# A decode layer on one core: another form for the load of x, and another pad ahead of the buffers

## The chip, the cores and the metric

The kernel runs on one core of one Trainium2 chip. The metric is the time of one execution on the device in microseconds. Before the change the median of three runs is 193.54 us (193.43 to 193.62).

## What is computed

One token (x is 1 x 1 x 512, bf16) goes through a layer norm. From the normed x come an attention over the last 4096 positions of a cache with 32 heads of 128, and a small MLP with two inner products whose result gates the attention's output. All inputs are bf16.

```python
def _A_ref(x, k_cache, v_cache, wq, wo):
    W = min(4096, max(256, Sk // 4))            # 4096
    q = (x @ wq).reshape(B, Sq, Hq, Dh).transpose(0, 2, 1, 3)
    k = k_cache[:, :, Sk - W:, :]
    v = v_cache[:, :, Sk - W:, :]
    scores = jnp.einsum("bhqd,bhkd->bhqk", q, k) * (Dh ** -0.5)
    o = jnp.einsum("bhqk,bhkd->bhqd", _softmax(scores), v)
    return o.transpose(0, 2, 1, 3).reshape(B, Sq, Hq * Dh) @ wo

def _B_ref(x, w1, w2, w3, w4):
    ...
    x1 = x + hs                                  # hs: shifted h @ w2; with one token the shift leaves zeros
    h2 = _gelu(_layernorm(x1) @ w3) @ w4
    return x1 + h2

xn = _layernorm(x)
s = _A_ref(xn, A_k_cache, A_v_cache, A_wq, A_wo)
g = _silu(_B_ref(xn, B_w1, B_w2, B_w3, B_w4))
return x + s * g
```

K and V of the window are 33.6 MB each, the weights that are read some 12 MB more.

## The kernel before

**Tiling.** The 32 heads are worked in 8 groups of `G = 4`. A group's K, and likewise its V, is one tile of 128 partitions x 128 positions x 128 numbers, 32 KB in each partition, 4.19 MB in all. K has three buffers in `k_pool`, V two in `v_pool`. The pool `v_pool` is opened only when the second K group is through, in the place of the pool `wts`, which holds the weights of q and of the MLP and the tiles that are used at the start alone.

**x.** It is loaded twice: `x_bf` (L78, L79), spread as columns over 128 partitions with four numbers in each, and `x_row` (L80 to L82), as four rows of 128 in partitions 0, 32, 64 and 96 of a tile that GpSimd has cleared. `x_bf` is cast to `x_f` (L183) and goes into the layer norm (`ln_stats`, L158 to L179: two products with a matrix of ones on PE, the rest on DVE, one power on GpSimd). Out come `xn_f` and `xn_bf`. `x_row` is used by `xn_row` (L242) and for the output at the very end (L656).

**From x to q.** `xn_bf` is permuted by a product (`xq_ps`, L194, `xq_bf`, L196) and multiplied with `wq_sb` into two PSUM tiles `qr_ps` (L208), which are copied to `q_row` (L210 on ACT, L211 on DVE), spread to all partitions by a product with `sel` (L214) into `q_bc` (L216), and turned into `q_pair` (L218 to L226).

**The MLP** runs beside it: 16 small products with `w2_sb` (L233), a second layer norm, products with `w3_sb` (L252), Gelu on ACT (L255), products with `w4_sb` (L270), and the gate `g_row` (L280).

**The groups.** For 64 or 80 of a group's 128 columns DVE multiplies K with q (`prod`, L321) and sums (`S`, L323) in four parts; the others are transposed on PE (`pt`, L339), copied by ACT (`kt`, L342) and multiplied on PE (`sT`, L350). Softmax and the products with V (`ov`, L427) follow two groups behind. Of the last group V comes in three pieces, and the last piece is multiplied one position column at a time (`oT`, L461); then come the output rows with wo (`y_ps`, L155), the gate (L654), x (L656) and the store.

**Queues and order.** SP issues all loads of the caches and of most weights, in program order (`load`, L75, L76): `w2_sb`, `w3_sb`, `w4_sb` in two parts, K of group 0 in two halves, then K and V in turn. ACT's queue issues `x_bf`, `x_row` and `wq_sb`, in this order. Engines work in order, each on its own list. The setup up to the loop over the groups is put in order by a scheduler; from L529 on the order of PE, DVE and ACT is the one written out by hand. Each transfer counts up one of eight completion semaphores, which are given out in turn; a transfer that takes one over waits until the earlier transfer that had it has landed. In the kernel before, SP's second K half takes over that of `x_bf`, the second K group that of `w2_sb`, the third that of `x_row`. The constants of the setup (`ident_bf`, `sel`, `perm`, and the masks of `make_masks`, L128 to L141) are made by GpSimd and DVE.

**Places in memory.** Pools lie behind one another. The pool `small` begins with a tile `pad` of 192 bytes (L71), then `x_bf` (8 bytes, which take 32), then `x_row` and the rest; behind `small` lie the pool `sm` and then `wts` or `v_pool`. `k_pool` lies ahead of them all.

Of the kernel before, what the change touches and what calls it, by code (L numbers as in the profile page):

```python
# [8 lines left out]
P = 128  # L9
BF16 = mybir.dt.bfloat16  # L10
FP32 = mybir.dt.float32
ACT = mybir.ActivationFunctionType
ALU = mybir.AluOpType
AX = mybir.AxisListType
# [12 lines left out]
def kernel(  # L27
# [14 lines left out]
    nc = tc.nc  # L42

    Bb, Sq, D = A_x.shape
    assert Bb == 1 and Sq == 1, "decode kernel: B == Sq == 1"
    _, H, Sk, Dh = A_k_cache.shape
    HD = A_wq.shape[1]
# [6 lines left out]
    KC = D // P  # L54
# [9 lines left out]
    small = ctx.enter_context(tc.tile_pool(name="small", bufs=1))  # L64
    ps_misc = ctx.enter_context(tc.tile_pool(name="ps_misc", bufs=1, space=PSUM))
# [2 lines left out]
    ps_o = ctx.enter_context(tc.tile_pool(name="ps_o", bufs=1, space=PSUM))  # L68
    ps_y = ctx.enter_context(tc.tile_pool(name="ps_y", bufs=1, space=PSUM))
    sm_pool = ctx.enter_context(tc.tile_pool(name="sm", bufs=3))  # L70
    small.tile([P, 96], BF16, name="pad")  # L71
    wts_guard = tc.tile_pool(name="wts", bufs=1)
    wts = wts_guard.__enter__()

    def load(dst, src):  # L75
        return tc.keep_in_program_order(nc.sync.dma_start(out=dst, in_=src))  # L76

    x_bf = small.tile([P, KC], BF16, name="x_bf")  # L78
    nc.scalar.dma_start(out=x_bf[:], in_=A_x.rearrange("a b (p c) -> p (a b c)", p=P))  # L79
    x_row = small.tile([P, P], BF16, name="x_row")  # L80
    nc.gpsimd.memset(x_row[:], 0.0)
    nc.scalar.dma_start(out=x_row[0:P:32, :], in_=A_x.rearrange("a b (j n) -> (a b j) n", j=KC))  # L82
    wq_sb = wts.tile([P, KC, HD], BF16, name="wq_sb")
    nc.scalar.dma_start(out=wq_sb[:].rearrange("p c n -> p (c n)"),
                        in_=A_wq.rearrange("(a b c) n -> b a (c n)", a=4, c=KC))
    w2_sb = wts.tile([P, KC, D], BF16, name="w2_sb")
    load(w2_sb[:], B_w2.rearrange("(p c) n -> p c n", p=P))
    w3_sb = wts.tile([P, KC, F], BF16, name="w3_sb")
# [14 lines left out]
    ident_bf = const.tile([P, P], BF16, name="ident_bf")  # L103
# [54 lines left out]
    def ln_stats(src_f, tag):  # L158
        ps = ps_misc.tile([P, KC], FP32, tag="misc", name="ln_ps")
        nc.tensor.matmul(ps[:], lhsT=ones_f[:], rhs=src_f, start=True, stop=True)  # L160
        tot = small.tile([P, 1], FP32, name=f"ln_tot_{tag}")
        nc.vector.reduce_sum(out=tot[:], in_=ps[:], axis=AX.X)
        negmean = small.tile([P, 1], FP32, name=f"ln_negmean_{tag}")
        nc.vector.tensor_scalar(out=negmean[:], in0=tot[:], scalar1=-1.0 / D,
                                scalar2=None, op0=ALU.mult)
        xc = small.tile([P, KC], FP32, name=f"ln_xc_{tag}")
        nc.vector.tensor_scalar(out=xc[:], in0=src_f, scalar1=negmean[:], scalar2=None,
                                op0=ALU.add)
        sq = small.tile([P, KC], FP32, name=f"ln_sq_{tag}")
        nc.vector.tensor_tensor(out=sq[:], in0=xc[:], in1=xc[:], op=ALU.mult)  # L170
        ps2 = ps_misc.tile([P, KC], FP32, tag="misc", name="ln_ps2")
        nc.tensor.matmul(ps2[:], lhsT=ones_f[:], rhs=sq[:], start=True, stop=True)
        vtot = small.tile([P, 1], FP32, name=f"ln_vtot_{tag}")
        nc.vector.reduce_sum(out=vtot[:], in_=ps2[:], axis=AX.X)
        rstd = small.tile([P, 1], FP32, name=f"ln_rstd_{tag}")
        nc.vector.tensor_scalar(out=rstd[:], in0=vtot[:], scalar1=1.0 / D,
                                scalar2=LN_EPS, op0=ALU.mult, op1=ALU.add)
        nc.gpsimd.tensor_tensor(out=rstd[:], in0=rstd[:], in1=neg_half[:, 0:1], op=ALU.pow)
        return xc, negmean, rstd  # L179


    x_f = small.tile([P, KC], FP32, name="x_f")
    nc.vector.tensor_copy(out=x_f[:], in_=x_bf[:])  # L183
    xc, negmean, rstd = ln_stats(x_f[:], "x")
    xn_f = small.tile([P, KC], FP32, name="xn_f")
    nc.vector.tensor_scalar(out=xn_f[:], in0=xc[:], scalar1=rstd[:], scalar2=None, op0=ALU.mult)
# [16 lines left out]
    for b in range(2):  # L203
        zeros(qr[b][:])
        for c in range(KC):
            wc = wq_sb[:, c, :].rearrange("p (g a d) -> p g a d", a=G, d=Dh)
            for a in range(G):
                nc.tensor.matmul(qr[b][32 * a:32 * a + 1], lhsT=xq_bf[:, c:c + 1], rhs=wc[:, 4 * b:4 * b + 4, a, :],  # L208
                                 start=False, stop=(c == KC - 1), skip_group_check=True)
    nc.scalar.copy(out=q_row[:, 0:4, 0, :], in_=qr[0][:])  # L210
    nc.vector.tensor_copy(out=q_row[:, 4:8, 0, :], in_=qr[1][:])  # L211
    for b in range(2):
        qb_ps = ps_tr.tile([P, 4, Dh], FP32, tag="pt", name="qb_ps")
        nc.tensor.matmul(qb_ps[:], lhsT=sel[:].rearrange("k b a -> k (b a)"), rhs=q_row[:, 4 * b:4 * b + 4, 0, :],  # L214
                         start=True, stop=True)
        nc.scalar.copy(out=q_bc[:, 4 * b:4 * b + 4, :], in_=qb_ps[:])  # L216
    for b in range(2):
# [5 lines left out]
        for t in range(2):  # L223
            rows = slice(64 * t, 64 * t + 64)
            nc.scalar.copy(out=q_pair[rows, 4 * b:4 * b + 4, :, G * t:G * t + G].rearrange("p g l a -> p g a l"),  # L225
                           in_=qt_ps[rows].bitcast(BF16).rearrange("p g (a m l) -> p g a m l", a=G, l=2)[:, :, :, 0, :])  # L226
# [4 lines left out]
    for j in range(KC):  # L231
        for c in range(KC):
            nc.tensor.matmul(hs_ps[:, j:j + 1], lhsT=w2_sb[:, c, j::4],  # L233
                             rhs=shifted_bf[:, c:c + 1], start=(c == 0), stop=(c == KC - 1))
# [30 lines left out]
    for i in range(11):  # L265
        n = P if i < 10 else 96
        terms.append((a_bf[0:n, i % 3, i // 3:i // 3 + 1], w4_sb[0:n, i, :]))
    for i, (col, w) in enumerate(terms):
        r = 32 * (i % 4)
        nc.tensor.matmul(hr_ps[r:r + 1].rearrange("r j n -> r (j n)"), lhsT=col, rhs=w, start=False,  # L270
                         stop=(i >= len(terms) - 4), skip_group_check=True)
# [25 lines left out]
                            op=ALU.max)  # L297
    par_t = const.tile([1 + G, PB, G], FP32, name="par_t")
    nc.vector.tensor_scalar(out=par_t[:],
                            in0=ident_f[0:1 + G, 1:1 + G].unsqueeze(1).to_broadcast([1 + G, PB, G]),  # L300
# [387 lines left out]
```

## Time and profile before

| | |
|---|---|
| median of three runs | 193.54 us (193.43 to 193.62) |
| the profiled execution | 193.37 us |
| its span, from the first to the last instruction | 191.2 us |
| busy: PE / DVE / ACT / GpSimd | 121.2 / 150.9 / 89.5 / 2.4 us |
| moved by DMA | 79.02 MB, 413 GB/s over the span |
| issue of `x_bf` to landing | 4.0 us |
| issue of `wq_sb` to landing | 17.5 us |
| issue of a whole K or V group to landing, median | 31.0, 30.6 us |

The profile is of one execution. The span leaves out what lies before the first and after the last instruction of the program, 2.2 us here. Queues in the profile are named by number; q1 is SP's, q10 ACT's, q8 carries the program's own instructions.

```profile
q1 hardware_dynamic: 4264, 74.65, 91.6%
q10 hardware_dynamic: 296, 4.20, 5.1%
q8 instruction: 9, 0.15, 0.3%
```

The columns are packets, MB, and the time that the packets took as a share of 16 engines over the span.

### The profile page before, as it was taken

The numbers are of one execution on the slowest core, as the hardware profiler recorded it, in microseconds if no ns is written. First come the engines' busy times: TensorE is split into PE (matmuls) and PEld (weight loads), VectorE is DVE, ScalarE is ACT, GpSimd is POOL, SyncE is SP. The second block draws the span as 40 slices with busy tenths as digits, with TensorE's granted clock in tenths as the row PEclk, the third lists the DMA queues.
The fourth block names the chain that finished last, engine by engine and source line by source line (L and its number), as shares of the span: only waits on it lengthen the run. The fifth ranks groups of instructions, "written<-read, shape, count | busy, mean of one in ns | idle before, by whom it ended". The sixth has DMA issues, their size and how long they took to land.

```text
span 191.2 us, 2843 instructions
## 1 busy us (share of the span) xinstructions
PE 121.2 (63%) x1161; PEld 77.0 (40%) x1161; DVE 150.9 (79%) x175; ACT 89.5 (47%) x191; POOL 2.4 (1%) x11
## 2 busy tenths in 40 slices
PE   1554853989826368356945773681889289749772
PEld 0430222767615334243434432540764078513321
DVE  1560169979999999999999999999999997990111
ACT  2001270887795076527364654552575147743120
POOL 2110000000000000000000000000000000000000
PEclk9999696555665556955585579558555855996999
DMA  6999999999999999999999999999999998999990
GB/s 202 436 444 410 431 425 432 439 439 437 432 440 432 432 428 439 439 439 418 428 418 425 439 428 408 456 432 435 439 439 434 428 432 379 471 435 394 415 372 29
DMA packets 4572, 79.02 MB, mean 413 GB/s; under 512 B 624, under 2 KB 1232, under 8 KB 1488
## 3 DMA queue, kind: packets, MB, share of 16 engines
q1 hardware_dynamic: 4264, 74.65, 91.6%
q10 hardware_dynamic: 296, 4.20, 5.1%
q8 instruction: 9, 0.15, 0.3%
q14 instruction: 3, 0.02, 0.0%
HBM read 78.84 MB, written 0.00 MB: 412 GB/s over the span
## 4 chain that ended last, share of the span: by engine, by line
DVE 47%; DMA 42%; PE 6%; ACT 1%; issue 1%; SPq 1%; DVEq 0%; ACTq 0%
DMA kv<-in_A_k_cache_dram 31%; DVE S L323 28%; DVE prod L321 16%; DMA kv<-in_A_v_cache_dram 9%; PE pt L339 3%; DMA x_bf<-in_A_x_dram 2%; ACT kt L342 1%; PE ov L427 1%; PE sT L350 1%; DVE m L366 1%; SPq L76 1%; DVE S L364 1%; DVE mx L374 1%; PE oT L461 1%; PE ot_ps L444 0%
## 5 line engine op out<-in xcount | busy, mean ns | idle before, releaser
L323 DVE TENSOR_REDUCE S<-prod 128x20 f32<-128x2560 bf16 (+1 forms) x32 | 86.0, 2686 | 1.1
L342 ACT COPY kt<-pt 128x1024 bf16<-128x1024 bf16 x52 | 51.4, 1013 | 40.0 <-PE pt L339 38.1
L339 PE MATMUL pt<-ident_f,kv 128*128 128x128 f32 x208 | 49.2, 392 | 10.0 <-DMA kv<-in_A_k_cache_dram 10.0
L321 DVE TENSOR_TENSOR prod<-kv,q_bc 128x2560 bf16<-128x2560 bf16 (+1 forms) x32 | 45.4, 1417 | 3.6 <-ACT q_pair L225 1.8
L339 PEld LDWEIGHTS pt<-ident_f,kv 128*128 128x128 f32 x208 | 36.2, 205 | 13.9 <-DMA kv<-in_A_k_cache_dram 9.3
L350 PE MATMUL sT<-q_pair,kt 128*128 128x8 bf16 x416 | 19.6, 170 | 14.9 <-ACT kt L342 14.8
L350 PEld LDWEIGHTS <-kt 128*128 128x128 bf16 x416 | 16.9, 105 | 26.1 <-ACT kt L342 24.9
L427 PE MATMUL ov<-kv,pT 128*16 128x512 bf16 x248 | 23.2, 536 | 1.2 <-DMA kv<-in_A_v_cache_dram 1.2
L388 ACT ACTIVATE pT<-S,mb 128x128 bf16<-128x128 f32 x32 | 13.9, 572 | 0.3
L372 PE MATMUL mt_ps<-ident_f,m 128*1 128x128 f32 x8 | 2.9, 360 | 16.6 <-DVE rden L399 16.1
L433 ACT COPY ov_sb<-ov 128x512 f32<-128x512 f32 x8 | 4.7, 586 | 18.4 <-PE ov L427 18.4
L427 PEld LDWEIGHTS <-pT 128*16 128x16 bf16 x248 | 6.9, 112 | 14.3 <-issue 12.7
L359 ACT ACTIVATE own<-sT,par 128x48 f32<-128x48 f32 (+1 forms) x32 | 7.5, 356 | 3.7 <-PE sT L350 3.7
L444 PE MATMUL ot_ps<-ident_f,ov_sb 128*128 128x128 f32 x32 | 7.5, 379 | 2.2 <-ACT mb L384 1.7
L211 DVE CAST q_row<-qr_ps 128x512 bf16<-128x512 f32 x1 | 0.7, 692 | 10.0 <-PE qr_ps L208 10.0
L388 ACT ACTIVATION_READ_ACCUMULATOR pT<-S,mb 128x1 f32 x32 | 8.3, 258 | 0.0
L372 PEld LDWEIGHTS mt_ps<-ident_f,m 128*1 128x1 f32 x8 | 0.6, 80 | 17.1 <-DVE rden L399 16.4
L399 DVE RECIPROCAL rden<-den_ps 128x4 f32<-128x4 f32 x8 | 1.4, 175 | 6.7 <-PE den_ps L394 6.7
L381 PE MATMUL mb_ps<-md,par_t 5*128 5x4 f32 x16 | 3.9, 311 | 4.1 <-DVE md L376 4.1
L255 ACT ACTIVATE a_row<-a_ps 128x384 bf16<-128x384 f32 x1 | 0.5, 491 | 12.1 <-remote 12.1
L444 PEld LDWEIGHTS ot_ps<-ident_f,ov_sb 128*128 128x128 f32 x32 | 4.8, 188 | 3.2 <-ACT mb L384 2.1
L208 PE MATMUL qr_ps<-wq_sb,xq_bf 128*1 128x512 bf16 x32 | 3.5, 611 | 3.6 <-DMA wq_sb<-in_A_wq_dram 3.6
(122 smaller groups left out, 82.8 us busy)
## 6 DMA issues: line engine op xcount, KB each, us to landing
kv<-in_A_k_cache_dram SPq DMA_DIRECT2D x7, 4096.0 KB, 31.0
kv<-in_A_v_cache_dram SPq DMA_DIRECT2D x7, 4096.0 KB, 30.6
wq_sb<-in_A_wq_dram ACTq DMA_DIRECT2D x1, 4096.0 KB, 17.5
kv<-in_A_k_cache_dram SPq DMA_DIRECT2D x2, 2048.0 KB, 27.5
wo<-in_A_wo_dram SPq DMA_DIRECT2D x1, 2048.0 KB
kv<-in_A_v_cache_dram SPq DMA_DIRECT2D x1, 2048.0 KB
kv<-in_A_v_cache_dram SPq DMA_DIRECT2D x2, 1024.0 KB, 16.3
w_sb<-in_B_w_dram SPq DMA_DIRECT2D x1, 1376.0 KB, 10.3
```

Of the source, the lines that this page charges most:

```text
L208: nc.tensor.matmul(qr[b][32 * a:32 * a + 1], lhsT=xq_bf[:, c:c + 1], rhs=wc[:, 4 * b:4 * b + 4, a, :], start=False, stop=(c == KC - 1), sk ...
L321: nc.vector.tensor_tensor(out=prod[:, 0:m, :], in0=kn[:, rows, :], in1=q_bc[:, g:g + 1, :].to_broadcast([P, m, Dh]), op=ALU.mult)
L323: nc.vector.tensor_reduce(out=st[g]["S"][:, rows], in_=prod[:, 0:m, :], axis=AX.X, op=ALU.add)
L339: nc.tensor.transpose(pt[:, i, :], kn[:, c:c + 2, :].rearrange("p c d -> p (c d)").bitcast(FP32), ident_f[:])
L342: nc.scalar.copy(out=kts[b][:, 0:n, :], in_=pt[:, 0:n, :].bitcast(BF16))
L350: nc.tensor.matmul(st[g]["sT"][:, c:c + 2, :].rearrange("p c a -> p (c a)"), lhsT=kt[:, i, l::2], rhs=q_pair[:, g, l, :], start=(l == 0), ...
L359: nc.scalar.mul(s["own"][:, 0:m, a], s["sT"][:, 0:m, a], par[:, a:a + 1])
L381: nc.tensor.matmul(mb_ps[:], lhsT=par_t[:].rearrange("k b a -> k (b a)"), rhs=md[:], start=True, stop=True)
L388: nc.scalar.activation(out=s["pT"][:, :, a], in_=s["S"][:], func=ACT.Exp, scale=scale, bias=mb[:, a:a + 1], accum_out=s["sum"][:, a:a + 1])
L427: nc.tensor.matmul(ov[r:r + 4 * G], lhsT=s["pT"][:, c:c + 4, :].rearrange("p i a -> p (i a)"), rhs=v[:, c:c + 4, :], start=(i < 4), stop=( ...
L433: nc.scalar.copy(out=s["ov_sb"][:], in_=ov[:])
L444: nc.tensor.transpose(ot_ps[:, step * j:step * j + P], s["ov_sb"][:, j, :], ident_f[:])
```

## The change

x for the columns is loaded as 16 rows of 32 numbers (64 bytes) into `x_in`, in 16 partitions. A product with `x_up`, a 0/1 matrix of 16 x 128, puts row r on the eight partitions 8r to 8r+7 (`x_all`, 128 x 32 in PSUM); the mask `x_own` keeps in each partition the four numbers that belong to it, the other 28 become zero (`x_pick`), and a sum over the eight pieces gives `x_f`. The cast L183 goes. On ACT's queue `wq_sb` now stands ahead of `x_row`. The pad grows from 192 to 416 bytes, and `x_in` takes 64 bytes where `x_bf` took 32. The new tiles `x_up`, `x_own` and `x_pick` lie in `wts`, behind the weights.

```diff
-    small.tile([P, 96], BF16, name="pad")
+    small.tile([P, 208], BF16, name="pad")
...
-    x_bf = small.tile([P, KC], BF16, name="x_bf")
-    nc.scalar.dma_start(out=x_bf[:], in_=A_x.rearrange("a b (p c) -> p (a b c)", p=P))
+    XR, XC = 16, D // 16
+    x_in = small.tile([XR, XC], BF16, name="x_in")
+    nc.scalar.dma_start(out=x_in[:], in_=A_x.rearrange("a b (r n) -> (a b r) n", r=XR))
+    wq_sb = wts.tile([P, KC, HD], BF16, name="wq_sb")
+    nc.scalar.dma_start(out=wq_sb[:].rearrange("p c n -> p (c n)"),
+                        in_=A_wq.rearrange("(a b c) n -> b a (c n)", a=4, c=KC))
     x_row = small.tile([P, P], BF16, name="x_row")
     nc.gpsimd.memset(x_row[:], 0.0)
     nc.scalar.dma_start(out=x_row[0:P:32, :], in_=A_x.rearrange("a b (j n) -> (a b j) n", j=KC))
-    wq_sb = wts.tile([P, KC, HD], BF16, name="wq_sb")
-    nc.scalar.dma_start(out=wq_sb[:].rearrange("p c n -> p (c n)"),
-                        in_=A_wq.rearrange("(a b c) n -> b a (c n)", a=4, c=KC))
...
+    m8 = P // XR
+    x_up = wts.tile([XR, XR, m8], BF16, name="x_up")
+    nc.vector.tensor_copy(out=x_up[:], in_=ident_bf[0:XR, 0:XR].unsqueeze(2).to_broadcast([XR, XR, m8]))
+    x_own = wts.tile([P, m8], BF16, name="x_own")
+    nc.vector.tensor_reduce(out=x_own[:], in_=ident_bf[:].rearrange("d (i t) -> d t i", t=m8), axis=AX.X, op=ALU.max)
+    x_all = ps_misc.tile([P, m8, KC], FP32, tag="misc", name="x_all")
+    nc.tensor.matmul(x_all[:].rearrange("p t c -> p (t c)"), lhsT=x_up[:].rearrange("k r t -> k (r t)"), rhs=x_in[:],
+                     start=True, stop=True)
+    x_pick = wts.tile([P, m8, KC], FP32, name="x_pick")
+    nc.vector.tensor_tensor(out=x_pick[:], in0=x_all[:], in1=x_own[:].unsqueeze(2).to_broadcast([P, m8, KC]), op=ALU.mult)
     x_f = small.tile([P, KC], FP32, name="x_f")
-    nc.vector.tensor_copy(out=x_f[:], in_=x_bf[:])
+    nc.vector.tensor_reduce(out=x_f[:], in_=x_pick[:].rearrange("p t c -> p c t"), axis=AX.X, op=ALU.add)
```

## The prediction

> **What bounds the kernel now.** I read the page's slices first, then the chain that ended last, then busy time by stretch, then the first microseconds. The page (slices of 4.78 us, and the summed chain):
>
> ```profile
> DVE  1560169979999999999999999999999997990111
> ...
> DMA  6999999999999999999999999999999998999990
> ...
> DVE 47%; DMA 42%; PE 6%; ACT 1%; issue 1%; SPq 1%; DVEq 0%; ACTq 0%
> ```
>
> The chain names DVE first, but the DMA row is at 9 in every slice between the first and the last. An engine can be on the chain and still not set the time, if what it releases only joins a queue. So the pieces of the chain, in order of time (start, length, what):
>
> ```profile
> 0.74 4.03 DMA x_bf<-in_A_x_dram
> ...
> 5.36 36.62 DMA kv<-in_A_k_cache_dram
> ...
> 42.08 1.50 DVE prod L321
> ...
> 130.42 23.05 DMA kv<-in_A_k_cache_dram
> ...
> 168.94 17.25 DMA kv<-in_A_v_cache_dram
> 186.19 0.05 issue
> 186.24 0.97 PE oT L461 x32
> ```
>
> The K load that DVE releases at 130.42 lands 23.05 us later. Its own 4.19 MB take 9.7 us at the 434 GB/s of the table below, so 13.3 us of older transfers lay ahead of it. The first half of the last V load is issued at 167.70 and by the trace's landings is complete at 181.31: 13.6 us, less 4.8 us for its 2.1 MB, leaves 8.8 us ahead of it. That is the smallest lead I find. DVE, PE and ACT may thus be late by up to 8.8 us before the DMA engines run dry. Busy time by stretch (stretch, length, busy time of five rows of engines, PE clock, DMA share, GB/s):
>
> ```profile
> 0.00:2.00 2.00, 0.61 (x1) 0.10 (x1) 0.52 (x6) 0.00 (x0) 1.24 (x9) 1.00 0.39 33
> 2.00:4.00 2.00, 0.00 (x0) 0.00 (x0) 0.00 (x0) 1.08 (x1) 0.00 (x0) 1.00 0.80 275
> 4.00:6.00 2.00, 0.59 (x2) 0.50 (x2) 0.48 (x3) 0.20 (x1) 0.00 (x0) 1.00 1.03 428
> ...
> 42.00:130.00 88.00, 55.23 (x540) 37.48 (x539) 86.86 (x66) 49.85 (x113) 0.00 (x0) 0.62 1.01 434
> ```
>
> The transfers run at 428 to 434 GB/s from 4 us on, and the only stretch with bytes missing is the first 4 us. The span is therefore: first packet at 1.78, then 79 MB as fast as the 16 engines move them, last V bytes at 186.19, then a fixed tail of 5.0 us to 191.2. The profiled execution took 193.37 us, 2.2 us more than its span; the median of the runs is 193.54, 0.17 above it.
>
> **The change, part by part.**
>
> *x for the columns.* The trace has 128 packets of 8 bytes for `x_bf`, 9 ns each, between 2.17 and 4.24 us, mixed one by one with the 4096-byte packets of `w2_sb`. I take one packet for each of the 16 new rows, as there is one for each of the 128 old ones. Busy time saved: 112 x 9 ns / 16 engines = 0.06 us. Of the 96 `w2_sb` packets that start between 2.8 and 5 us, most take 159 ns, but ten exceed 200 ns, and the excess over 159 ns is 1.52 us in sum, 0.10 us per engine; if all of it is the small packets' doing it goes too. Bounds: nothing, if the 9 ns hide in the neighbours' time; 0.87 us, if the small load also makes the stall at the very start (13 first packets of `w2_sb` at 750 to 1134 ns and three behind the first small packets at 551 to 756 ns, 0.71 us per engine over 159 ns). Against the far end: all of those 13 started before the first `x_bf` packet did (2.17). I take the 0.06 and half of the 0.10: **-0.11 us**. A loss I exclude down to 0.03 us: a 64-byte packet lies between the 9 ns of 8 bytes and the 18 ns of `x_row`'s 256.
>
> *The product and the mask* replace the cast of `x_f` (L183, 0.17 us):
>
> ```profile
> 4.79 0.17 DVE L183 CAST x_f<-x_bf 128x4 f32<-128x4 bf16 x1 [3.45 <-DMA x_bf<-in_A_x_dram]
> ...
> 8.69 0.16 PE L194 MATMUL xq_ps<-xn_bf,perm 128*128 128x4 bf16 x1 [0.57 <-DVE x_f L236]
> ...
> 25.93 1.23 DVE L321 TENSOR_TENSOR prod<-kv,q_bc 128x2048 bf16<-128x2048 bf16 x1 [1.80 <-ACT q_pair L225]
> ...
> 42.08 1.49 DVE L321 TENSOR_TENSOR prod<-kv,q_bc 128x2560 bf16<-128x2560 bf16 x1 [1.32 <-DMA kv<-in_A_k_cache_dram]
> ```
>
> The matmul lies between the 0.16 us of L194 (128x4) and the 0.27 of L149 (128x128), the mask from PSUM between 0.15 (L236, 128x4) and 0.34 (L242, 128x128), the sum between 0.16 (L162) and 0.28 (L131): 0.47 to 0.89 us in place of 0.17. The two constants `x_up` (like `sel`, 0.28) and `x_own` (like `mt`, 0.38) need only the identity and fill DVE's 3.45 us of waiting for x. x itself should be there by about 3.4 us (the first packets end near 2.9, and the last of `x_bf` took 0.5 us from 4.24 to its landing at 4.76), so `x_f` is ready near 4.2 instead of 4.96. On the built order the scheduler then mixes the mask builders of L131 to L139 into the layernorm, which gives part of this back. None of it counts: the first product starts at 25.93, its K half lands at 25.83, and before 42.08 DVE stands idle for 1.32 us for the next K. Price now **0**; without the 8.8 us of queued transfers, each us of delay past 1.32 would cost one.
>
> *wq ahead of x_row.* ACT's queue no longer holds `wq_sb` behind the memset and `x_row` (issued at 2.29 now, about 1.2 then). The same bytes go out of the same engines, so **0** for the stream. What moves: wq's 32 KB packets (1213 ns) alternate with SP's packets, so `w2_sb` may land as late as 10 us (2.9 + 5 packets x 1.37 + 0.4) instead of 4.6, `w3_sb` near 17 instead of 11.5, wq itself by 15 to 19 instead of 19.8. PE works in order: the products with `w2_sb` (L233) stand ahead of `xq_ps`, those with `w3_sb` (L252, 2.9 us) ahead of `qr_ps`. q can start near 20, as now. In the built order ACT has one more table load (1.28 us) and the Gelu (0.49) between the first copy of `q_row` and `q_bc`: some 0.9 us later there. First product at 25.9 to 27.5, inside the covers named. On SP's queue the completion counters are shared out anew: the third K load (now at 6.70, behind `x_row`'s landing) waits for wq, the second (5.36) still for `w2_sb`. Behind SP's wait stand only later K and V loads. When wq lands at, say, 19 us the ring still holds 8.3 MB (11.7 MB of weights and two K groups, less some 3.4 MB moved), 19 us of work. `x_row`, now behind wq, is read by `xn_row`, which the built order has after the layernorms and right ahead of the cast of `qr_ps` (L211), which starts at 23.36 now and itself needs wq. Cost 0 as well.
>
> *The pad.* Behind the two tiles everything in `small` and above moves by (416 + 64) - (192 + 32) = 256 bytes, so no buffer changes its place modulo 256; in the built program the V buffers and weights begin at multiples of 256 before and after, the K buffers 128 bytes off both times. **0**; a gain is bounded by the packets: 81 of 83 V packets between 71.5 and 78 us take the shortest time of 1213 ns, so there is nothing to lose there. The Trainium skill ("DMA: Bandwidth & Descriptors", section "How a descriptor splits into AXI transactions") says that a transfer piece that does not start on a 256-byte boundary costs extra beats. By that rule a 32 KB packet 128 bytes off has 1028 beats for 1024, an estimate of 0.4%, and the trace agrees: 50 of the 80 K packets between 33 and 39 us take 1218 ns or more. If V and weights had been off and were now mended, the sum by it would be about 0.4 us lower; hence the rival below.
>
> Sum: 193.37 - 0.11 = 193.26 for an execution like the profiled one, and 193.54 - 0.11 = **193.43** for the median. I call same what lies within 0.2%, 0.39 us, about what a measurement here can tell from no change.
>
> **The rivals.**
> 1. *The stall at the start goes with the small packets.* For: three first packets stalled directly behind an `x_bf` packet. Against: thirteen did before there was one. From half to all of the 0.87 us: 192.7 to 193.1.
> 2. *The pad does what its words say*, though the residues do not change: 5 ns of 1213 on the 42 MB of V, weights and late wo rows, 97.5 us of stream: 0.40 us more, 193.0. Against: the 1213 ns of V now.
> 3. *A program fetch strikes the slowest DMA engine (slower).* The trace has nine 16 KB packets on the instruction queue, eight before the last V byte. Each takes 1.02 to 1.30 us, mostly with a neighbour stretched by some 0.45 us, on one engine. The last V piece lands on six engines at 184.2 to 184.6, on ten at 185.3 to 186.2, so the engines struck once already set the end. One struck twice would add some 1.5 us: 195.0. It decides from the ninth fetch coming before 186.2 and on such an engine; it comes at 187.21 now, 20 us after the one before, and three more PE instructions hardly move it. The Trainium skill ("Runtime: NRT & Kernel Launch", "Instruction fetch mechanics") has 256 instructions in such a block, by which three would make an estimated 0.2 us.
> 4. *The compute side becomes late by more than the queue is deep.* `w2_sb` and `w3_sb` later than I reckon, PE's order carrying it to q; the price is what goes beyond 8.8 us. Landings would have to be 10 us worse than the bounds above: 194.5.
>
> **How the numbers follow.** My forecast 0.74, its own range 193.15 to 193.75; rival 1 0.14, rival 2 0.03, rival 3 0.06, rival 4 0.03. Faster by over 0.2% (below 193.15): most of rival 1, rival 2 and an edge of the forecast, 0.18. Slower: rivals 3 and 4 and an edge, 0.10. Same: 0.72. The range 192.85 to 193.9 holds the forecast, rival 2 and over half of rival 1.
>
> **What would show it.** Right: the DMA row at 9 throughout; the last V landing within 0.3 us of 186.19 in a span near 191.1; 16 packets for x; `x_f` earlier by up to 1 us and the first product not earlier than 25.9; wq landed before 19.8, SP's third K issue right behind it, later `w2_sb`. Wrong: 4096-byte packets without the 0.7 us stall and the stream ahead by that much from 4 us on (rival 1); V packets below 1213 ns (rival 2); a ninth 16 KB packet before the end, one engine 1.5 us behind the others (rival 3); a hole in the DMA row after 130 us (rival 4).

## The result, and the profile after

Before, 193.39 us (median of 18 runs, 193.17 to 193.62); after, 193.03 us (18 runs, 192.81 to 193.64). The ratio is 0.9981 [0.9974, 0.9988]: 0.36 us faster. The interval leaves no doubt of a gain, and it lies just inside the 0.2% (0.39 us) that the prediction calls no change. The 193.03 is 0.40 below the predicted 193.43, but 0.15 of that is the kernel before itself: the prediction starts from the 193.54 of three runs, and the 18 runs beside the changed kernel gave 193.39. The profiled execution took 193.06 us with a span of 191.0.

The page of the kernel after, the slices of 4.78 us and the summed chain:

```profile
DVE  5720259969999999999999999999999999980111
DMA  6999999999999999999999999999999999999990
...
DVE 62%; DMA 30%; PE 3%; issue 1%; ACT 1%; SPq 1%; DVEq 0%; ACTq 0%
```

The DMA row is at 9 throughout, as before. The summed chain has moved from DMA to DVE, 47% to 62%, and the time has hardly moved: where two conditions come true almost together a small shift changes which pieces such a chain counts, so its shares are not used here as a measure of what sets the end. The end of the chain, in order of time (start, length, what):

```profile
4.17 37.67 DMA kv<-in_A_k_cache_dram
42.33 1.50 DVE prod L332
...
169.68 16.36 DMA kv<-in_A_v_cache_dram
186.04 0.05 issue
186.09 0.97 PE oT L472 x32
```

It still ends with the last V load and the fixed tail, 0.15 us earlier than before (186.04 for 186.19). The second K group is issued at 4.17 instead of 5.36. Before, SP stood with the K half ahead of it until `x_bf` had landed (4.76); now that half goes at 3.37, behind `x_in`'s landing at 3.36, and the group waits for `w2_sb` alone (landed at 4.15). It lands at 41.84 instead of 41.98: of the 1.19 us only 0.14 are left behind the queue of older loads. The stretches show where the 0.15 us comes from (stretch, length, busy time of five rows of engines, PE clock, DMA share, GB/s), kernel after:

```profile
0.00:2.00 2.00, 0.87 (x2) 0.13 (x2) 0.94 (x9) 0.00 (x0) 1.23 (x9) 1.00 0.16 20
2.00:4.00 2.00, 0.18 (x1) 0.10 (x1) 0.95 (x6) 1.05 (x1) 0.00 (x0) 1.00 0.89 330
...
42.00:130.00 88.00, 54.87 (x538) 37.71 (x535) 86.62 (x66) 49.56 (x112) 0.00 (x0) 0.62 1.01 433
```

In the first 4 us 2 x 20 + 2 x 330 = 700 KB are moved instead of 2 x 33 + 2 x 275 = 616 KB: 84 KB, or 0.19 us at 432 GB/s. Counted packet by packet without the program's own, the lead is 0.25 us at 4 us, 0.19 at 8, and 0.14 from 20 us to 184. The rest of the stream runs at the same rate. The timeline of the kernel after shows the new steps (start, length, engine, line, operation; in brackets the idle time before and what ended it):

```profile
3.40 0.18 PE L189 MATMUL x_all<-x_in,x_up 16*128 16x32 bf16 x1 [1.54 <-DMA x_in<-in_A_x_dram]
...
3.62 0.19 DVE L192 TENSOR_TENSOR x_pick<-x_all,x_own 128x32 f32<-128x32 f32 x1 [1.05 <-PE x_all L189]
...
3.92 0.19 DVE L194 TENSOR_REDUCE x_f<-x_pick 128x4 f32<-128x32 f32 x1
...
25.88 1.23 DVE L332 TENSOR_TENSOR prod<-kv,q_bc 128x2048 bf16<-128x2048 bf16 x1 [3.10 <-DMA kv<-in_A_k_cache_dram]
```

Three instructions of 0.18 to 0.19 us do what the cast did, and `x_f` is ready at 4.11 instead of 4.96. The first product starts at 25.88, 0.05 us earlier, and waits for K now: the 0.85 us are gone into a wait.

The span's part is thus near 0.2 us. The rest does not lie in the span at all. Every run gives its time and its span; the difference is what the device spends ahead of the first and behind the last instruction. Means over the runs (of the kernel before the three sets that ran beside the experiments, on three chips, as its 18 runs above have no span on record):

| kernel | runs | time | span | outside the span |
|---|---|---|---|---|
| before, three times | 32 / 28 / 19 | 193.39 / 193.28 / 193.40 | 191.22 / 191.11 / 191.22 | 2.17 / 2.17 / 2.18 |
| after | 18 | 193.03 | 191.02 | 2.01 |

The error of a mean is some 0.04 us for the time and 0.02 for the part outside. So 0.20 us were gained in the span and 0.16 outside it; on one chip with the kernel before (`e4_after_again` below) it is 0.21 and 0.19. One execution of `e12_k_aligned_x_behind`, 195.41 us for 192.47 of its fastest, was in the slower state and is left out of its means and its ratio. The prediction treated the 2.2 us outside as fixed.

### The profile page after: what moved, and what is told of

It is laid out like the page before. It is cut to its first block, busy times and chain, and to the rows that moved or that the text cites. A ratio compares the mean times of both kernels' runs of the same rounds, so it can differ in the third digit from the quotient of the medians.

```text
span 191.0 us, 2851 instructions
## 1 busy us (share of the span) xinstructions
PE 120.9 (63%) x1162; PEld 76.0 (40%) x1162; DVE 151.9 (80%) x178; ACT 90.4 (47%) x192; POOL 2.3 (1%) x11
## 4 chain that ended last, share of the span: by engine, by line
DVE 62%; DMA 30%; PE 3%; issue 1%; ACT 1%; SPq 1%; DVEq 0%; ACTq 0%
DVE S L334 38%; DMA kv<-in_A_k_cache_dram 20%; DVE prod L332 19%; DMA kv<-in_A_v_cache_dram 9%; DMA w_sb<-in_B_w_dram 2%; PE ov L438 2%; DVE m L377 1%; DVE S L375 1%; ACT kt L353 1%; SPq L76 1%; DVE mx L385 1%; PE oT L472 1%; DVE md L387 0%; DVE oT L461 0%; DVE ox L509 0%
## 5 line engine op out<-in xcount | busy, mean ns | idle before, releaser
L350 PE MATMUL pt<-ident_f,kv 128*128 128x128 f32 x208 | 47.5, 381 | 9.3 <-DMA kv<-in_A_k_cache_dram 9.3
L350 PEld LDWEIGHTS pt<-ident_f,kv 128*128 128x128 f32 x208 | 35.0, 200 | 12.9 <-DMA kv<-in_A_k_cache_dram 10.7
L438 PE MATMUL ov<-kv,pT 128*16 128x512 bf16 x248 | 24.0, 553 | 0.7 <-DMA kv<-in_A_v_cache_dram 0.7
L221 ACT CAST q_row<-qr_ps 128x512 bf16<-128x512 f32 x1 | 0.6, 585 | 15.6 <-PE qr_ps L219 15.6
L392 PEld LDWEIGHTS mb_ps<-md,par_t 5*128 5x128 f32 x16 | 3.8, 291 | 5.3 <-PE sT L361 3.6
```

Of the source, the lines that this page charges most:

```text
L350: nc.tensor.transpose(pt[:, i, :], kn[:, c:c + 2, :].rearrange("p c d -> p (c d)").bitcast(FP32), ident_f[:])
L392: nc.tensor.matmul(mb_ps[:], lhsT=par_t[:].rearrange("k b a -> k (b a)"), rhs=md[:], start=True, stop=True)
L438: nc.tensor.matmul(ov[r:r + 4 * G], lhsT=s["pT"][:, c:c + 4, :].rearrange("p i a -> p (i a)"), rhs=v[:, c:c + 4, :], start=(i < 4), stop=( ...
```

## The experiments

Two questions: what gained 0.2 us in the span, and what the 0.16 outside. For the first, A1 is rival 1 (the stall of the first `w2_sb` packets belongs to the small packets among them), and A2 says that the stall is `w2_sb`'s own and that x's packets cost by their number. Two further experiments then ask whether they cost the same wherever they stand. Differences of means below are to the kernel before in the same set of runs.

**One part at a time.** `e1_rows_only` has the new load, product and mask, but the old order on ACT's queue:

```diff
     nc.scalar.dma_start(out=x_in[:], ...)
-    wq_sb = wts.tile(...); nc.scalar.dma_start(out=wq_sb[:]..., in_=A_wq...)
     x_row = small.tile(...); nc.gpsimd.memset(x_row[:], 0.0); nc.scalar.dma_start(out=x_row[0:P:32, :], ...)
+    wq_sb = wts.tile(...); nc.scalar.dma_start(out=wq_sb[:]..., in_=A_wq...)
```

> The changed kernel with ACT's queue in the old order (x_in, x_row, wq_sb). Theory A (the lead is made by the 16 packets in place of 128 in the first 4 us): all of the gain stays, 0.25 to 0.45 us under the kernel before, stream ahead by some 0.25 us at 4 us. Rival B (wq issued earlier makes it): no gain, within 0.1 us. Rival C (the shift by 256 bytes makes it): gain stays, but then the pad alone has it too.

`e2_order_only` is the kernel before with `wq_sb` put ahead of `x_row`'s clearing and load:

```diff
     nc.scalar.dma_start(out=x_bf[:], ...)
+    wq_sb = wts.tile(...); nc.scalar.dma_start(out=wq_sb[:]..., in_=A_wq...)
     x_row = small.tile(...); nc.gpsimd.memset(x_row[:], 0.0); nc.scalar.dma_start(out=x_row[0:P:32, :], ...)
-    wq_sb = wts.tile(...); nc.scalar.dma_start(out=wq_sb[:]..., in_=A_wq...)
```

> The kernel before with wq_sb ahead of x_row on ACT's queue and nothing else. Theory A: within 0.1 us of the kernel before. Rival B: 0.25 to 0.45 us faster. Rival C: no change.

`e3_pad_only` is the kernel before with the buffers moved by 256 bytes:

```diff
-    small.tile([P, 96], BF16, name="pad")
+    small.tile([P, 224], BF16, name="pad")
```

> The kernel before with the pad longer by 256 bytes, which moves every later buffer as the change does. Theory A and rival B: within 0.1 us of the kernel before. Rival C: 0.25 to 0.45 us faster.

`e4_after_again` is the changed kernel beside these three, with no edit.

> The changed kernel itself once more, on the same chip as the three parts: 0.25 to 0.50 us under the kernel before by every theory; it gives the size that the parts have to add up to.

| | median | ratio [95%] | span | outside |
|---|---|---|---|---|
| rows only | 192.91 | 0.998 [0.9971, 0.9989] | -0.17 | -0.23 |
| order only | 193.34 | 1.0 [0.9991, 1.0009] | 0.00 | -0.02 |
| pad only | 193.27 | 0.9997 [0.9988, 1.0006] | -0.07 | +0.02 |
| changed kernel again | 192.97 | 0.9978 [0.9969, 0.9988] | -0.21 | -0.19 |

(Span and outside: means less those of the kernel before.) The load in rows with its product and mask has the whole gain, in the span and outside it. The order alone and the pad alone have none that can be told from nothing. The same stretches, of rows only:

```profile
0.00:2.00 2.00, 0.87 (x2) 0.13 (x2) 0.94 (x9) 0.00 (x0) 1.23 (x9) 1.00 0.20 29
2.00:4.00 2.00, 0.18 (x1) 0.10 (x1) 0.81 (x5) 1.06 (x1) 0.00 (x0) 1.00 0.90 328
```

and of order only:

```profile
0.00:2.00 2.00, 0.61 (x1) 0.10 (x1) 0.52 (x6) 0.00 (x0) 1.23 (x9) 1.00 0.42 31
2.00:4.00 2.00, 0.00 (x0) 0.00 (x0) 0.00 (x0) 1.05 (x1) 0.00 (x0) 1.00 0.77 268
```

714 KB and 598 KB in 4 us, against 616 before: the lead goes with the rows alone.

**Stall or number of packets.** `e7_x_behind_w2` takes x's packets out from among the first ones of `w2_sb`: `x_in` goes on SP's queue right behind it.

```diff
-    nc.scalar.dma_start(out=x_in[:], in_=A_x.rearrange("a b (r n) -> (a b r) n", r=XR))
...
     load(w2_sb[:], ...)
+    load(x_in[:], A_x.rearrange("a b (r n) -> (a b r) n", r=XR))
```

> The changed kernel with x_in on SP's queue behind w2_sb, so that no x packet lies among the first packets of w2_sb. Theory A1 (the stall of the first packets is made by x's packets between them): the excess of w2_sb's packets over 159 ns falls from 0.4 to 0.6 us per engine to under 0.2, and the stream gains another 0.2 us. Theory A2 (the stall is w2_sb's own start, x adds only by the number of its packets): excess stays at 0.4 to 0.6, time within 0.1 us of the changed kernel, 193.0.

193.02 us, 0.9986 [0.9978, 0.9995], span -0.17, outside -0.16: the same as the changed kernel. The time of `w2_sb`'s packets over 159 ns is 0.37 us per engine with no x packet near them and 0.39 in the changed kernel. What is left of the stall there belongs to `w2_sb` itself, against A1. With the 128 small packets it was 0.81 in the profiled execution of before, so a half did go with them. Over all profiled executions the stall is 0.56 to 0.86 in five kernels with them (mean 0.71) and 0.12 to 0.59 in nine without (mean 0.35). But the lead does not follow it from one kernel to the next: the changed kernel taken again has a stall of 0.59, rows only of 0.46, the changed kernel of 0.39, and they lead by 0.19, 0.19 and 0.25 us at 4 us; `e5_k_aligned` below has a stall of 0.12 alone and leads by 0.20. In the changed kernel the lead grows over the time in which the kernel before has its small packets, from 0.05 us at 2.5 to 0.25 at 4.0.

`e9_both_loads` is the changed kernel with the old load of 8-byte packets put back ahead of the new one, its result unread. (The pad shrinks so that all places stay.)

```diff
-    small.tile([P, 208], BF16, name="pad")
+    small.tile([P, 192], BF16, name="pad")
...
+    x_bf = small.tile([P, KC], BF16, name="x_bf")
+    nc.scalar.dma_start(out=x_bf[:], in_=A_x.rearrange("a b (p c) -> p (a b c)", p=P))
     nc.scalar.dma_start(out=x_in[:], ...)
```

> The changed kernel with the old load of 128 rows of 8 bytes added at its old place, first on ACT's queue, into a tile that nothing reads. Theory A (the packets make the difference): the whole gain goes, 193.3 to 193.45 us, stream at 4 us back to that of the kernel before, and the 2.0 us outside the span back to 2.17. Rival D (what replaces the cast, or the order that the scheduler makes of it, gives part of it): part of the gain stays, 193.1 to 193.2.

193.54 us, 1.0015 [1.0006, 1.0024]. The lead is gone: 0.09 us at 4 us, none at 6, and 0.08 behind the kernel before at 184. So the small packets take the lead back, with the product and the mask still in place. The time is worse than a mere return (0.25 us behind the kernel before in the mean), and the stream explains only a part of that. In the profiled execution (193.80, span 191.8 for 191.2) the last V lands at 186.40, 0.21 later than before, and PE comes to it 0.46 us later still:

```profile
186.86 0.95 PE oT L474 x32
```

In how many of the other ten executions PE was late is not on record, so the time of this kernel does not price the packets; its lead does.

`e10_late_128` issues the same load on SP's queue behind the V load of group 2, where the stream runs full:

```diff
-    small.tile([P, 208], BF16, name="pad")
+    small.tile([P, 192], BF16, name="pad")
...
+        if cache is A_v_cache and g == 2:
+            x_bf = small.tile([P, KC], BF16, name="x_bf")
+            load(x_bf[:], A_x.rearrange("a b (p c) -> p (a b c)", p=P))
```

> The changed kernel with the old load of 128 rows of 8 bytes added on SP's queue at the fifth K group, far from the start. If the cost of the 8-byte rows is one of their number anywhere: 0.2 to 0.4 us slower than the changed kernel, and the time outside the span back to 2.17 us. If it is one of their place among the first packets: within 0.1 us of the changed kernel inside the span.

193.24 us, 0.9998 [0.9989, 1.0007]: the gain is lost, and in the mean it is 0.33 us behind `e7_x_behind_w2` on the same chip. In the profiled execution, however, the packets came between 97.6 and 99.3 us, and between 96 and 110 us the stream lost 0.09 us, from 0.10 ahead of the changed kernel to 0.01. That is 11 ns for each of the eight packets of an engine. The profiled execution (193.06) is the fastest of its eleven; what the slower ones lost is not shown.

`e8_small_midstream` takes 1536 such packets, 96 for each engine, in two loads of 768:

```diff
-    small.tile([P, 208], BF16, name="pad")
+    small.tile([P, 112], BF16, name="pad")
...
+        if cache is A_v_cache and g in (1, 3):
+            x_many = small.tile([P, 6, 2 * KC], BF16, name=f"x_many{g}")
+            load(x_many[:, :, 0:KC], A_x.rearrange("a b (p c) -> p (a b) c", p=P).to_broadcast([P, 6, KC]))
```

> The changed kernel with 1536 packets of 8 bytes added on SP's queue at the third and the fifth K group, 768 each, twelve times the old load, far from the start; nothing reads them. If a small packet costs what its record shows (9 ns on one of 16 engines): 0.86 us slower than the changed kernel, 193.85 us. If it costs as much anywhere as the old load did in the whole (some 0.25 us for 112 packets, 36 ns on its engine): 3.4 us slower, 196.4. If it hides among the large packets: 193.0.

198.65 us, 1.0262 [1.0231, 1.0292], above all three values expected. In the profiled execution (197.03) the stream falls 3.0 us behind the changed kernel, 31 ns for each packet of an engine in the mean. But the mean hides two prices. The stretches in which the two loads ran, this kernel:

```profile
78.00:84.00 6.00, 0.88 (x12) 0.74 (x12) 5.93 (x7) 1.33 (x2) 0.00 (x0) 0.59 0.71 241
118.00:124.00 6.00, 3.33 (x41) 2.61 (x38) 5.97 (x4) 3.05 (x4) 0.00 (x0) 0.50 0.99 392
```

and the same stretches of the changed kernel:

```profile
78.00:84.00 6.00, 0.81 (x12) 0.50 (x11) 5.93 (x7) 1.49 (x2) 0.00 (x0) 0.83 1.01 437
118.00:124.00 6.00, 3.01 (x33) 2.47 (x33) 5.97 (x4) 2.02 (x2) 0.00 (x0) 0.62 1.03 442
```

At 78 us the DMA share falls to 0.71: engines stand without a packet, down to 5.5 of 16 at work at 78.8 us, and the load costs 2.7 us, 56 ns for each of its 48 packets on an engine. At 118 us packets of 16 KB are mixed with the small ones, the share stays at 0.99, and the load costs 0.33 us, 7 ns a packet, about what the records say. So A2 in its simple form, one price for each packet, falls as well: 7 to 11 ns where the engines stay at work, 56 where they run dry. Why they ran dry at 78 us is open. At the start the 112 packets saved are worth 0.14 to 0.25 us, 20 to 36 ns for each of the seven on an engine if the whole lead is theirs, between the two. And the 3.0 us explain the larger part of the lost time only: against the changed kernel the span grew by 4.0 us in this execution and by 5.4 in the mean. In this execution the rest lies in how unevenly the engines end. The last V lands at 189.87, 3.83 us later, and counted packet by packet 4.1 of the 16 engines are still at work in the microsecond from 190, for 1.0 from 187 in the changed kernel. What the slower executions lost beyond that was not found.

**The places in memory.** `e6_old_pad` keeps the pad at 192 bytes, so that `x_in`'s 64 bytes put V and the weights 32 bytes past a multiple of 256:

```diff
-    small.tile([P, 208], BF16, name="pad")
+    small.tile([P, 96], BF16, name="pad")
```

> The changed kernel with the pad left at 192 bytes, so that V buffers and weights begin 32 bytes off a multiple of 256 (what the larger x tile alone would have done). If a start off 256 costs as in the K packets: 32 KB packets of V at about 1218 ns, 0.3 to 0.5 us slower than the changed kernel, the whole gain over the kernel before gone (193.3 to 193.5). If not: 193.0.

193.95 us, 1.0029 [1.0017, 1.0041]: 0.92 us behind the changed kernel (+0.56 against -0.36 in the means), about twice what was expected. `e5_k_aligned` goes the other way and puts K at a multiple of 256 as well:

```diff
+    lead = ctx.enter_context(tc.tile_pool(name="lead", bufs=1))
+    lead.tile([P, 64], BF16, name="lead_pad")
...
-    small.tile([P, 208], BF16, name="pad")
+    small.tile([P, 144], BF16, name="pad")
```

> The changed kernel with 128 bytes ahead of the K pool and the pad shorter by as much, so that the K buffers too begin at multiples of 256 bytes and nothing else moves against 256. If a start off 256 costs transfer time: K packets of 32 KB at 1213 ns throughout, a few ns less on average, 0.15 to 0.45 us under the changed kernel, about 192.7 us. If it does not: the same as the changed kernel within 0.1 us, about 193.0 us.

192.63 us, 0.9964 [0.9952, 0.9976], the best of all: span -0.53 where the changed kernel has -0.20. The ends of the chains, old pad first, then K aligned:

```profile
170.36 16.64 DMA kv<-in_A_v_cache_dram
187.04 0.97 PE oT L472 x32
```

```profile
168.33 17.33 DMA kv<-in_A_v_cache_dram
185.70 0.97 PE oT L474 x32
```

The last V load lands at 187.00 and 185.66, against 186.04. The packets account for most of it. Of the 80 packets of 32 KB between 33 and 39 us, where K is loaded, 51 took 1218 ns or more in the kernel before (the prediction counted 50); with K aligned all 80 take 1213. With the old pad none of the 89 packets of that size between 71.5 and 78 us, where V is loaded, takes 1213; most take 1216, some 1224. Summed over all sizes and per engine, the time over the shortest of each size from 1 to 32 KB (4 KB left out, the stall) is 0.67 us in the changed kernel, 0.44 with K aligned and 1.46 with the old pad: 0.79 of the 0.96 us by which the last V lands later with the old pad, and 0.23 of the 0.39 by which it lands earlier with K aligned. The Trainium skill ("DMA: Bandwidth & Descriptors", section "How a descriptor splits into AXI transactions") counts extra beats for a descriptor that does not start on a 256-byte boundary, by which a packet 128 bytes off would take an estimated 0.4% longer; the 1218 ns for 1213 agree. For 32 bytes off the same count gives one beat in 1024, an estimated 0.1%, and there the measured 1216 to 1224 ns are 0.2 to 0.9%; so the page's count does not give the whole price, and why it is higher is open.

`e12_k_aligned_x_behind` has the edits of `e5_k_aligned` and `e7_x_behind_w2` together.

> The changed kernel with K at multiples of 256 bytes and x_in on SP's queue behind w2_sb, the two experiments that kept or raised the stream's lead, together. By the lead of the stream (0.26 us more from K, 0.1 more from x): 0.35 to 0.5 us under the changed kernel, 192.5 to 192.7 us, under both kernels. If the end is set by PE's chain instead: no better than K alone.

192.79 us over all seven executions, and a ratio of 0.9968 [0.9957, 0.998] without the one of 195.41: not to be told from the 0.9964 of K aligned alone. The profiled streams differ in the sense expected (a lead of 0.47 us for 0.39 at 184, the last V at 185.57 for 185.65), by too little to show in the time.

**The part outside the span.** All kernels with the product and the mask have it at 1.94 to 2.04 us; the kernel before, order only and pad only have 2.15 to 2.19. `e9_both_loads` has the old load back and still 2.04, so the load is not it. `e11_more_program` tries the length of the program: the kernel before, with some unread work behind the cast of x.

```diff
     nc.vector.tensor_copy(out=x_f[:], in_=x_bf[:])
+    spare = wts.tile([P, 4], FP32, name="spare")
+    for i in range(3):
+        nc.vector.memset(spare[:, i:i + 1], 0.0)
+    nc.scalar.copy(out=spare[:, 3:4], in_=ones_f[:, 0:1])
+    sp_ps = ps_misc.tile([P, KC], FP32, tag="misc", name="sp_ps")
+    nc.tensor.matmul(sp_ps[:], lhsT=zero_bf[:], rhs=zero_bf[:, 0:KC], start=True, stop=True)
```

> The kernel before with a few small instructions that nothing reads: three on VectorE, one product on TensorE, one copy on ScalarE (which brings a table load). Tests only the 0.15 us by which the time outside the span is less in every kernel with the product and mask. If it goes with the length of the program: 2.0 us outside the span for 2.17, and some 0.15 us under the kernel before. If with what the instructions do: 2.17 as before and the same time.

193.19 us, 0.9991 [0.9982, 0.9999]; the span in the mean 191.21 (before 191.22), outside 1.99 (before 2.18). A kernel with more work takes 0.2 us less in the mean, all of it outside the span. One mark goes with it. The queues between 189 and 196 us of this kernel (packets, MB, share of 16 engines):

```profile
q14 instruction: 1, 0.01, 0.3%
q1 hardware_dynamic: 8, 0.00, 0.1%
```

and of the kernel before:

```profile
q1 hardware_dynamic: 8, 0.00, 0.1%
```

The packet on q14, 8 KB some 1.8 us past the span's end, is in all kernels with the shorter time and in none of the three with the longer. That is a companion; which instruction asks for it, and why the time is shorter then, stays open. ACT's list is not it: in rows only the profile has 191 busy instructions on ACT, as in the kernel before, and yet the shorter time. Nor does `e11_more_program` part the length of the program from what the added instructions are.

## Why the prediction was right, point by point

**What bounds the kernel.** The stream of transfers does, in eleven of the fourteen profiled executions: the lead of 0.14 us at 184 us and the last landing 0.15 us earlier agree, and the places in memory move the end by what they do to the packets. The prediction's lead of 8.8 us for the compute side was too simple, though. It looked only at how early a load is issued. At the very end PE must also be through with what stands ahead of `oT`. In the kernel after PE waits 0.18 us for the last V, kernel after:

```profile
186.09 0.96 PE L472 MATMUL oT<-pT,kv 128*128 128x4 bf16 x32 [0.18 <-DMA kv<-in_A_v_cache_dram]
```

It was 0.18 before, too. In the profiled execution of `e7_x_behind_w2` the chain ends with PE instead:

```profile
182.18 0.97 PE ov L438 x16
...
186.30 0.95 PE oT L472 x32
```

There the last V had landed at 185.82 and PE came 0.5 us later. The granted clock of the stretch from 154 to 166 us (the number ahead of the last two) is lower than in the kernel after, second line:

```profile
154.00:166.00 12.00, 10.95 (x107) 8.80 (x109) 10.68 (x11) 8.28 (x10) 0.00 (x0) 0.50 1.01 431
154.00:166.00 12.00, 9.65 (x118) 7.20 (x120) 11.43 (x12) 8.70 (x12) 0.00 (x0) 0.78 0.99 422
```

It is 0.50 in just three of the profiled executions, those of `e7_x_behind_w2`, `e9_both_loads` and `e11_more_program`, and in these three alone PE comes 0.45 to 0.5 us behind the last V. In the other eleven the clock is 0.60 to 0.81 there, and `oT` starts within 0.05 us of V's landing. So the end is a near tie, in which a gain of the stream can be lost to PE in one execution and not in another. This may be why spans of one kernel scatter by several tenths; that was not tried.

**The load of x, the term that was mis-sized.** "I take the 0.06 and half of the 0.10: -0.11 us" was measured as -0.20 in the span. The mechanism, fewer small packets, was right: the load with its product and mask alone has the gain (`e1_rows_only`), and with the old load back the stream's lead goes (`e9_both_loads`). The size was not: if the whole lead is theirs, the packets cost 20 to 36 ns each in this place instead of the 9 of their records. The far bound of 0.87 us falls with `e7_x_behind_w2`: 0.37 us of the stall are there without any small packet near. Of rival 1 its lower end is half true: about half of the stall does go with the small packets, but the lead at 4 us is 0.25 us at most, less than the 0.44 at which that rival begins. That 193.03 lies within its 192.7 to 193.1 does not speak for it, since 0.16 us of the gain is outside the span and 0.15 of the distance is the kernel before's own. How much of the 0.25 is the stall's and how much the small packets' own time is not settled. A part of the lead, 0.25 down to 0.14, goes by 20 us. With x behind `w2_sb`, where `wq_sb`'s first packet comes at 3.55 us instead of 5.31, 0.23 are left at 20 us; the cause is not shown.

**The 2.2 us outside the span** had no term. The prediction sets the execution's 193.37 beside the span and the median, but nothing in its sum asked whether a longer program changes what lies around the span. It gave 0.16 us, nearly half of the gain. This is what the sum left out, and its cause stays open. That the gain of 0.36 us still stayed under the 0.39 that the prediction calls the same is luck: 193.03 is below the forecast's own range of 193.15 to 193.75, and only the wide range, which was to take in rivals 1 and 2, holds it.

**The product and the mask** at 0: right. They took 0.18 + 0.19 + 0.19 = 0.56 us, within 0.47 to 0.89, and `x_f` came 0.85 us earlier (predicted up to 1). The cover held: DVE's first product waits for K.

**wq ahead of x_row** at 0: right, `e2_order_only` has a ratio of 1.0. `wq_sb` landed at 18.66 (19.83 before), SP's third K load went at 18.68 right behind it, and the first product came at 25.88, by 0.02 before the stated 25.9. The fear for `w2_sb` was wrong: it landed at 4.15, earlier than the 4.59 of before, because the first packet of `wq_sb` came only at 5.31, when `w2_sb` was through. `w3_sb` did land later, 13.87 for 11.45, and nothing waited.

**The pad** at 0: right for the comparison asked, as V and the weights stay at multiples of 256 (`e3_pad_only`), and rival 2 falls. But the pad isn't idle: without it the 64 bytes of `x_in` would have turned 0.36 us of gain into 0.56 of loss (`e6_old_pad`). The prediction had the rule for K's packets and didn't ask what the change would cost with the old pad.

**Rivals 3 and 4:** no ninth program fetch before the end, no hole in the DMA row. (In the kernel before, the ninth fetch came 16.5 us after the eighth, at 187.2 after 170.7, not 20 as the prediction has it; the rival does not hang on that.)

## What to carry to other kernels

Where transfers bound a kernel, look at the start byte of every tile that a DMA fills before touching anything else: 32 bytes off cost 0.9 us here, and moving K by 128 bytes gained some 0.3, nearly as much as the whole change. Few-byte packets are best avoided even when their records look free, and their price has to be measured in their place. And compare spans and times apart: a difference of 0.2 us can lie wholly outside the span, with no part in what the added instructions compute.

## What was unexpected of the hardware

- A longer program had 0.16 to 0.2 us less outside its span (1.99 for 2.18 us with unread work added).
- 768 packets of 8 bytes cost the stream 2.7 us in one place and 0.33 in another of the same execution; in the first, DMA engines stood idle though the next K load had been issued at 57.54 us.
- 32 bytes off a multiple of 256 cost not only the 32 KB packets (1216 to 1224 for 1213 ns, +0.30 us per engine over the run) but more than that again in those of 16 KB (+0.28) and of 8 to 11 KB (+0.13).
- The packets of the first large load lose 0.12 to 0.59 us per engine over their shortest time with no 8-byte packets among them, and 0.56 to 0.86 with.
- With the granted clock at 0.50 from 154 to 166 us (three profiled executions of fourteen) PE came 0.45 to 0.5 us late to the last V; with 0.60 to 0.81 it never did. Which of the two brings the other was not tried.
